# A linear-attention kernel with its layers: an empty GpSimd instruction in the drain's place, and the state's update in another visit

## The chip, the cores and the metric

One core of a Trainium2 chip. The metric is device time in microseconds (us) for one call; lower is better. The kernel before took 424.89 us (median of three runs, 424.53 to 431.61).

## The reference, cut to what matters

Inputs are float32 and already drawn: four batches, eight heads, 768 tokens, 48 features per head. First comes a recurrent attention with a decaying state, then three layers whose maximum is taken, then an output layer.

```
for t in range(S):
    cur = einsum('bhd,bhe->bhde', u[None] * kt, vt)
    y[:, :, t] = einsum('bhd,bhde->bhe', rt, state + cur)
    state = wt[:, :, :, None] * state + einsum('bhd,bhe->bhde', kt, vt)
...
h = max(max(x @ w1, x @ w2), x @ w3)      # 3072 x 384 by 384 x 768
return h @ w_out                          # 768 x 384
```

## The kernel before, in words

**Two streams of work share TensorE.** The attention runs over 24 chunks of 128 tokens (six chunks per batch). The layers run over six halves of 512 tokens. Four chunks make the input of one half, so the attention of half h+1 runs while the layers of half h do.

**The layers** (`moe_groups`) come in groups of nine matmuls, 26 groups to a half: 18 of L147 (six feature blocks by w1, w2, w3; each feeds one PSUM bank, tile `psm`) and 8 of L167 (the output layer). `take_up` frees a bank: for w1 ScalarE copies it (L126), for w2 and w3 VectorE takes the maximum (L129). It is written one group late: the take-up of a group stands in its engine's queue behind what was written while that group and the gap after it were emitted. The pool `ps_m` has three banks, and a new tile gets the bank that was freed longest ago, in the order of the program.

**The attention** is a list of lettered steps, one chunk at a time; the string `ORD` (L71) orders them for chunks 4 to 23. A digit after a letter is how many chunks ahead the step works, `|` ends a unit, and one unit is emitted after nearly every layer group. The letters that matter here:

- R (`from_state`, L450): state times r, into the tile y. V (`values`, L489): half of the values, added into y. Z (`values2`, L489 again): the other half, which adds into the same banks from the other half of the array's rows; a TensorE drain (L482) stands before it. E (`result`, L503): ScalarE copies y into x.
- X (`scores`, L417): the next chunk's products into the tiles `gram`. M: VectorE takes them into `a`.
- T (`transposes`, L437): four transposes of the next chunk's keys into the one bank of the pool `ps_tu`, and a ScalarE copy of it to `kn` (L439), of which there is one.
- U (`to_state`, L460): keys times values into the same bank of `ps_tu`, read from `kn`. S (`state`, L473 and L475): VectorE forms the next state from it. Every sixth chunk (5, 11, 17, 23) ends a batch and has no U and no S, and the chunk after it starts from no state.
- b, f, r, c: the decays and what they scale, two chunks ahead (VectorE L335, L345, L356, L357; c is a ScalarE Square in place over what r reads, L362). d, e: the diagonal, two chunks ahead (GpSimd L373, L374, then VectorE L387 and GpSimd L393). n: a load.

So before the change a chunk has one long visit to TensorE (R, X, V, U, drain, Z), one short one four groups later (T), and VectorE's S, r and ScalarE's c between them. All engines run their own instructions in the order written (`manual_schedule`). From half 1 on the layers split their input into two fp32r parts on ScalarE and VectorE (`x_parts`, L106 and L107), emitted near the end of the half before; in half 1 the weights are split as well (`fix`); from half 2 on every second group carries a check of one weight block (L307 on VectorE, L309 on ScalarE).

Of the kernel before, what the change touches and what calls it, by code (L numbers as in the profile page):

```python
# [29 lines left out]
F32 = mybir.dt.float32  # L30
# [10 lines left out]
B, H, S, D = 4, 8, 768, 48  # L41
DM, FF = 384, 768
NP = 4
C = 128
# [6 lines left out]
HT = 512  # L51
HC = C // 2
CPH = HT // C
# [14 lines left out]
FRONT = "n2 w U0 b1 | d1 f1 r1 | w e1 c1 S0 W4 X1 T1 | R0 M0 | V0 Z0 E0 |"  # L68
LAST = "R0 M0 | V0 Z0 E0 n2 w U0 W9 n3 | b1 d1 | f1 r1 w | e1 c1 S0 X1 T1 R1 |"
TURN = "b1 d1 w | f1 w | r1 c1 | e1 M0 w | "  # L70
ORD = "w R0 X1 V0 U0 Z0 E0 b2 d2 | f2 n3 w | S0 r2 c2 | e2 M1 w | T1 w | |"  # L71


START = ("aaaaaaaaaaaacaaacaccaxmcacmcamcamcamcamcamcamcamcaamca"
# [10 lines left out]
def lines(n):  # L85

    return -(-n // LINE) * LINE
# [3 lines left out]
def kernel(ctx: ExitStack, tc, tin, nat, u_flat, u_pair, v_t, w_all, out, ytr):  # L91
    nc = tc.nc
# [83 lines left out]
    with ExitStack() as fast:  # L176
# [15 lines left out]
        ps_tu = pool("ps_tu", 1, space=PSUM)  # L192
        ps_m = pool("ps_m", 3, space=PSUM)
# [4 lines left out]
        natt = {}  # L198
# [230 lines left out]
        def goes_on(k):  # L429
            return k % NCH < NCH - 1  # L430

        def transposes(k):
            if goes_on(k):
                p = prep[k]
                pt = ps_tu.tile([128, 512], F32, name="tu")
                for pr in range(NP):
                    nc.tensor.transpose(pt[:, pr * 112:pr * 112 + 112], p["kp"][0:112, pr, :], ident[0:112, 0:112])  # L437
                p["kn"] = kn = kn_p.tile([128, lines(NP * 112)], F32, name="kn")[:, 0:NP * 112].rearrange("p (a b) -> p a b", a=NP)
                nc.scalar.copy(out=kn[:, :, :].rearrange("p a b -> p (a b)"), in_=pt[:, 0:NP * 112])  # L439
# [27 lines left out]
        def state(k):  # L467

            if goes_on(k):
                new = prep[k]["pu"][0:112, 0:NP * D].rearrange("p (a b) -> p a b", a=NP)  # L470
                if k % NCH > 0 and k >= CPH:
# [3 lines left out]
                nc.vector.tensor_tensor(out=sstar[(k + 1) % 2][0:112, :, 0:D], in0=new,  # L475
                                        in1=dec[(k + 1) % 2][0:112, :].unsqueeze(2).broadcast_to([112, NP, D]), op=ALU.mult)

        def values(k, second=False):
            p = prep[k]
            fresh = k % NCH == 0 and not second  # L480
            if second:
                nc.tensor.drain()  # L482
            for late in range(2):
                for row in range(2):
                    for half, m in ((0, 64), (1, 48)):
                        hh, j = row ^ second, (1 - row) ^ late
                        h, lo = 4 * half + 2 * j + hh, 64 * row
                        a = p["a"][lo:lo + HC, 2 * hh + half]
                        nc.tensor.matmul(p["y"][64 * half:64 * half + m, hh, j, HC * late:C],  # L489
                                         lhsT=natt[k][0][lo:lo + HC, h * D:h * D + m],  # L490
                                         rhs=a[:, j, :] if late else a[:, j::2 - j, :],
                                         start=fresh and not late, stop=True, skip_group_check=True)

        def values2(k):
            values(k, True)

        def result(k):
# [7 lines left out]
            for lo in (0, 64) if slot == CPH - 1 else ():  # L505
                for j in range(KT):
                    eng = nc.scalar if lo and half < PLAIN else nc.sync
                    eng.dma_start(out=x[lo + 48:lo + 64, j, :], in_=x[lo + 16 * j:lo + 16 * j + 16, KT, :])

        steps = dict(X=scores, M=take, T=transposes, R=from_state, U=to_state, S=state, V=values, Z=values2, E=result, n=load,  # L510
                     b=prep_scan_b, f=prep_scan_f, r=prep_rk, c=prep_check, d=prep_diag1, e=prep_diag2)
        ready = {("n", k) for k in range(3)}
# [16 lines left out]
        def attn():  # L529
            for step in "bdfeWrXTcW":  # L530
                ahead(step, 0) if step != "W" else warmer(2 if ("X", 0) in ready else 8)
            for k in range(NK):
                if k == CPH:
                    nc.scalar.dma_start(out=u_bc[:, :], in_=u_flat.partition_broadcast(128))
                for step in (FRONT if k < CPH - 1 else LAST if k < CPH else TURN + ORD if k == CPH else ORD).split():
                    if step == "|":
# [134 lines left out]
    with tc.If(verdict[0] != 0, label="general"), ExitStack() as slow:  # L671
# [9 lines left out]
        with tc.For_i(0, B) as b:  # L681
            for pr in range(NP):
# [18 lines left out]
                for j in range(KT):  # L701
                    with tc.For_i(0, 16) as i:
# [16 lines left out]
                        for q in range(2):  # L719
                            z = ps_z.tile([2, S // 2], F32, name="z")  # L720
                            nc.tensor.matmul(z[:, :], lhsT=sel[0:112, :], rhs=kv[0:112, q * (S // 2):(q + 1) * (S // 2)],
                                             start=True, stop=True)
                            nc.vector.tensor_copy(out=yo[:, q * (S // 2):(q + 1) * (S // 2)], in_=z[:, :])
                        for hh in range(2):
                            place, lo = 2 * hh + pr % 2, 64 * (pr // 2)
# [8 lines left out]
        for i in range(NW if w_all.dtype != F32 else 0):  # L734
# [3 lines left out]
            lo, hi = words[:, :, 0], words[:, :, 1]  # L738
# [93 lines left out]
```

## Time and profile before

| | |
|---|---|
| median of three runs | 424.89 us |
| the profiled execution, its own time | 423.95 us |
| its span, first to last instruction | 422.2 us |
| mean granted TensorE clock in it | 0.995 |
| TensorE busy, weight loads busy | 408.9 us (97%), 320.9 us (76%) |
| VectorE, ScalarE, GpSimd busy | 272.0, 151.9, 74.3 us |
| matmuls of the layers L147 and L167, share of the chain that ended last | 55% and 17% |

The busy share of TensorE counts matmuls whose ends are modelled, so the distance from one start to the next says more than a duration. An fp32 matmul shows as two rows. "issue" as a releaser means that an engine waited for nothing that the profile shows. PE is TensorE's matmuls, PEld its weight loads, DVE VectorE, ACT ScalarE, POOL GpSimd.

### The profile page before, as it was taken

What the parts mean: (1) busy time and instruction counts of PE and PEld (TensorE: products, weight loads), DVE (VectorE), ACT (ScalarE), POOL (GpSimd) and SP (SyncE); (2) the same over time, 40 slices, a digit from 0 to 9 for tenths busy, and PEclk for the clock granted to TensorE, in tenths of its full rate; (3) what the DMA queues carried; (4) which work ended last, traced back from release to release, by engine and by line L of the source; (5) the groups of instructions that cost most, each with busy time, mean ns of one, the idle gap of its engine ahead of it and who ended that gap; (6) DMA issues with size and microseconds to landing.
All of it is one profiled execution on the core that took longest, in us unless ns stands there. A gap on an engine that the chain in (4) does not pass through costs nothing.

```text
span 422.2 us, 9012 instructions
## 1 busy us (share of the span) xinstructions
PE 408.9 (97%) x3695; PEld 320.9 (76%) x3695; DVE 272.0 (64%) x515; ACT 151.9 (36%) x318; POOL 74.3 (18%) x92
## 2 busy tenths in 40 slices
PE   6989999999999999999999999999999999999995
PEld 3665545556678888987888988888988888988895
DVE  5988789877769977835867658658547624223320
ACT  1334344232554443424425455334523221312111
POOL 3120111030443140313023113113113100000000
PEclk9989999999999999999999999999999999999999
DMA  8835975244172403295735496653280000200002
GB/s 224 258 100 151 351 250 168 68 168 124 44 231 67 123 7 118 48 283 173 219 92 182 114 279 209 198 180 94 52 265 23 2 2 0 79 18 0 1 2 78
DMA packets 20702, 53.27 MB, mean 126 GB/s; under 512 B 2816, under 2 KB 9088, under 8 KB 20656
## 3 DMA queue, kind: packets, MB, share of 16 engines
q1 hardware_dynamic: 16832, 42.61, 33.3%
q10 hardware_dynamic: 3824, 10.03, 7.6%
q8 instruction: 30, 0.49, 0.5%
q14 instruction: 16, 0.13, 0.1%
HBM read 46.74 MB, written 4.72 MB: 122 GB/s over the span
## 4 chain that ended last, share of the span: by engine, by line
PE 92%; DVE 4%; issue 1%; DMA 1%; ACT 1%; POOL 0%; POOLq 0%; DVEq 0%; ACTq 0%
PE psm L147 55%; PE psm L167 17%; PE y L489 5%; PE gram L417 4%; PE y L450 3%; PE tu L460 3%; PE psm L526 2%; PE tu L437 2%; PE psm L383 1%; DMA out_dram<-m 1%; DVE tin L356 1%; DVE tin L357 1%; DVE gf L345 1%; DVE gf L335 1%; DVE x_lo L107 0%
## 5 line engine op out<-in xcount | busy, mean ns | idle before, releaser
L147 PE MATMUL psm<-x_hi,w 128*128 128x512 f32 x540 | 172.9, 394 | 0.6 <-ACT m L126 0.6
L147 PEld LDWEIGHTS psm<-x_hi,w 128*128 128x128 f32 x540 | 101.4, 188 | 22.5 <-ACT m L126 0.8
L147 PE MATMUL psm<-x_lo,w 128*128 128x512 f32 x270 | 105.3, 390 | 0.0
L129 DVE TENSOR_TENSOR m<-psm,m 128x512 f32<-128x512 f32 x60 | 41.2, 687 | 58.6 <-PE psm L147 52.6
L167 PE MATMUL psm<-w,h_hi 128*128 128x384 f32 x288 | 78.0, 364 | 0.0
L393 POOL TENSOR_SCALAR_AFFINE_SELECT a<-cs 64x512 f32<-64x512 f32 x48 | 35.5, 739 | 233.7 <-DVE cs L387 117.2
L147 PEld LDWEIGHTS psm<-x_lo,w 128*128 128x128 f32 x270 | 50.7, 188 | 9.9
L167 PEld LDWEIGHTS psm<-w,h_hi 128*128 128x128 f32 x288 | 51.8, 188 | 6.4
L147 PE MATMUL psm<-x,w 128*128 128x512 f32 x108 | 48.3, 598 | 0.0
L503 ACT COPY x<-y 112x512 f32<-112x512 f32 x24 | 14.1, 587 | 74.4 <-PE y L489 74.0
L167 PE MATMUL psm<-w,h_lo 128*128 128x384 f32 x120 | 40.2, 335 | 0.0
L362 ACT ACTIVATE gf<-gf 112x1034 f32<-112x1034 f32 x24 | 25.7, 1070 | 36.3 <-DVE tin L357 33.0
L106 ACT CAST h_hi<-m 128x512 fp32r<-128x512 f32 x30 | 18.7, 622 | 54.6 <-DVE m L129 54.6
L335 DVE TENSOR_TENSOR_SCAN gf<-tin,d_bwd 112x517 f32<-112x517 f32 x24 | 31.1, 1296 | 10.0 <-DMA tin<-in_tin_dram 10.0
L147 PEld LDWEIGHTS psm<-x,w 128*128 128x128 f32 x108 | 19.9, 190 | 22.8 <-issue 22.1
L107 DVE TENSOR_TENSOR h_lo<-m,h_hi 128x512 fp32r<-128x512 f32 x30 | 22.2, 740 | 19.0 <-ACT h_hi L106 19.0
L345 DVE TENSOR_TENSOR_SCAN gf<-tin,d_fwd 112x517 f32<-112x517 f32 x24 | 29.6, 1235 | 0.8
L489 PE MATMUL y<-a,v 64*64 64x128 f32 (+3 forms) x768 | 25.5, 248 | 2.9
L489 PEld LDWEIGHTS y<-a,v 64*64 64x64 f32 (+1 forms) x768 | 20.5, 126 | 6.0 <-issue 5.9
L373 POOL TENSOR_TENSOR kr<-kr 128x384 f32<-128x384 f32 x16 | 18.7, 1170 | 26.8 <-DMA kr<-in_nat_dram 25.8
L426 DVE COPY_PREDICATED a<-mask,gram 128x384 f32<-128x384 int32 x44 | 23.2, 582 | 0.0
L126 ACT COPY m<-psm 128x512 f32<-128x512 f32 x30 | 17.5, 582 | 15.9 <-PE psm L147 13.6
(71 smaller groups left out, 427.9 us busy)
## 6 DMA issues: line engine op xcount, KB each, us to landing
tin<-in_tin_dram SPq DMA_DIRECT2D x23, 677.7 KB, 5.5
w<-in_w_all_dram SPq DMA_DIRECT2D x24, 384.0 KB, 6.6
cv<-in_w_all_dram ACTq DMA_DIRECT2D x24, 384.0 KB, 3.3
kr<-in_nat_dram SPq DMA_DIRECT2D x16, 384.0 KB, 5.9
v<-in_nat_dram SPq DMA_DIRECT2D x24, 192.0 KB, 5.5
out_dram<-m SPq DMA_DIRECT2D x24, 192.0 KB, 2.3
x<-x SPq DMA_DIRECT2D x33, 32.0 KB, 2.0
tin<-in_tin_dram SPq DMA_DIRECT2D x1, 258.0 KB, 4.8
```

The lines of the kernel that those rows point to most:

```text
L106: nc.scalar.copy(out=hi, in_=src)
L107: rest = lambda: nc.vector.tensor_tensor(out=lo, in0=src, in1=hi.bitcast(F32), op=ALU.subtract)
L129: nc.vector.tensor_tensor(out=m[:, :], in0=ps[:, :], in1=m[:, :], op=ALU.max)
L147: nc.tensor.matmul(ps[:, :], lhsT=wt[f * 3 + wi][:, ct * 128:(ct + 1) * 128], rhs=xt[:, ct, :], start=(n == 0), stop=(n == KT * len(terms) ...
L167: nc.tensor.matmul(pss[tt][:, 0:DM], lhsT=ht[f][:, tok], rhs=wt[FT * 3 + f][:, :], start=(f == 0 and i == 0), stop=(f == FT - 1 and i == l ...
L335: nc.vector.tensor_tensor_scan(out=gf[0:112, 0, ::-1], data0=t[0:112, 0:WC][:, ::-1], data1=d_bwd[0:112, ::-1], initial=0.0, op0=ALU.mult, ...
L345: nc.vector.tensor_tensor_scan(out=gf[0:112, 1, :], data0=tbuf[k % NB][0:112, 0:WC], data1=d_fwd[0:112, :], initial=0.0, op0=ALU.mult, op1 ...
L362: nc.scalar.activation(out=flat, in_=flat, func=AF.Square, accum_out=acc[0:112, k:k + 1])
L373: nc.gpsimd.tensor_tensor(out=n[:, 0, :], in0=n[:, 0, :], in1=n[:, 1, :], op=ALU.mult)
L393: nc.gpsimd.affine_select(out=a[rows, :, 0:2, :], pattern=[[0, 4], [0, 2], [1, HC]], in_=cs[rows, :].rearrange("p (a b) -> p a b", b=2).un ...
L426: nc.vector.copy_predicated(out=p["a"][:, 2 * hh:2 * hh + 2, :, :].rearrange("p a b c -> p a (b c)"), mask=mask_b(2), data=p["gs"][hh].rea ...
L489: nc.tensor.matmul(p["y"][64 * half:64 * half + m, hh, j, HC * late:C], lhsT=natt[k][0][lo:lo + HC, h * D:h * D + m], rhs=a[:, j, :] if la ...
```

## The change

For chunks 4 to 23 the drain is left out. Instead GpSimd gets an empty instruction that waits for the last matmul of V, and the first matmul of Z waits for it. X moves between V and Z. U moves from the long visit to the unit that holds S, r and c, and T moves there too, two units earlier than it was. From chunk 5 on T takes a bank of the layers' pool, so that U and T need not share one.

```
-ORD = "w R0 X1 V0 U0 Z0 E0 b2 d2 | f2 n3 w | S0 r2 c2 | e2 M1 w | T1 w | |"
+ORD = "w R0 V0 X1 Z0 E0 b2 d2 | f2 n3 w | U0 T1 S0 r2 c2 | e2 M1 w | w | |"
...
         def transposes(k):
...
-                pt = ps_tu.tile([128, 512], F32, name="tu")
+                pt = ps_m.tile([128, HT], F32, name="psm") if k > CPH else ps_tu.tile([128, 512], F32, name="tu")
...
+        def after(later, sooner):
+            how = mybir.DependencyInfo(mybir.DependencyClass.Sync, mybir.DependencyReason.DATA)
+            tc.add_manual_dep(later.ins, sooner.ins.name, how, reason="the second values use the first's banks")
+            return later
...
         def values(k, second=False):
...
-            if second:
+            if second and k < CPH:
                 nc.tensor.drain()
...
-                        nc.tensor.matmul(p["y"][64 * half:64 * half + m, hh, j, HC * late:C],
+                        mm = nc.tensor.matmul(p["y"][64 * half:64 * half + m, hh, j, HC * late:C],
...
+                        if "first" in p:
+                            after(mm, p.pop("first"))
+            if not second and k >= CPH:
+                p["first"] = after(nc.gpsimd.nop(nofuse=True), mm)
```

## Rows read from the trace of the kernel before

**Rows 1.** The page, busy time: us (share of the span) xinstructions of each engine.
```profile
PE 408.9 (97%) x3695; PEld 320.9 (76%) x3695; DVE 272.0 (64%) x515; ACT 151.9 (36%) x318; POOL 74.3 (18%) x92
```
**Rows 2.** Waits of the whole span: us in total, times, longest.
```profile
PEld y L489 <- issue: 5.9, 24, 0.3
```
**Rows 3.** Timeline of TensorE, chunk 9's long visit: start, duration, work.
```profile
138.20 0.39 PE L147 MATMUL psm<-x_hi,w 128*128 128x512 f32 x1
138.52 0.66 PE L450 MATMUL y<-tin,sstar 48*64 48x128 f32 x16
139.02 0.84 PE L417 MATMUL gram<-tin 48*64 48x128 f32 x32
139.68 0.50 PE L489 MATMUL y<-a,v 64*48 64x128 f32 x16
140.12 0.67 PE L460 MATMUL tu<-v,kn 128*64 128x48 f32 x16
140.90 0.56 PE L489 MATMUL y<-a,v 64*64 64x128 f32 x16
141.39 0.50 PE L147 MATMUL psm<-x_hi,w 128*128 128x512 f32 x1
```
**Rows 4.** Timeline of the weight loads in the same visit, around the drain.
```profile
140.11 0.54 PEld L460 LDWEIGHTS tu<-v,kn 128*64 128x64 f32 x16
140.90 0.42 PEld L489 LDWEIGHTS y<-a,v 64*64 64x64 f32 x16 [0.24 <-issue]
```
**Rows 5.** Timeline of TensorE, chunk 11's visit, which has no U.
```profile
171.43 1.18 PE L489 MATMUL y<-a,v 64*48 64x128 f32 x32
172.54 0.62 PE L167 MATMUL psm<-w,h_hi 128*128 128x384 f32 x2
```
**Rows 6.** The chain that ended last, around chunk 13's T: start, us, line.
```profile
204.23 8.39 PE psm L147 x36
212.62 0.39 PE tu L437 x4
213.00 6.14 PE psm L147 x27
```
**Rows 7.** Timelines of VectorE and ScalarE, chunk 13: S, the Square, the take-up.
```profile
207.40 0.35 DVE L473 TENSOR_TENSOR scur<-tu,sstar 112x192 f32<-112x192 f32 x1
...
209.46 1.07 ACT L362 ACTIVATE gf<-gf 112x1034 f32<-112x1034 f32 x1 [0.95 <-DVE tin L357]
...
210.52 0.57 ACT L126 COPY m<-psm 128x512 f32<-128x512 f32 x1
```
**Rows 8.** Timelines of ScalarE and TensorE, chunk 12: a group that waited for its bank.
```profile
196.36 0.57 ACT L126 COPY m<-psm 128x512 f32<-128x512 f32 x1
...
196.98 0.50 PE L147 MATMUL psm<-x_hi,w 128*128 128x512 f32 x1 [0.62 <-ACT m L126]
```
**Rows 9.** Timelines of three engines, chunk 15 to the start of half 3.
```profile
235.76 0.36 DVE L473 TENSOR_TENSOR scur<-tu,sstar 112x192 f32<-112x192 f32 x1 [0.66 <-PE tu L460]
...
240.78 0.48 ACT L171 COPY m<-psm 128x384 f32<-128x384 f32 x1 [0.43 <-PE psm L167]
241.16 0.65 ACT L309 ACTIVATE cv<-cv,mid_top 128x384 f32<-128x384 uint32 x1
...
242.92 1.67 ACT L106 CAST x_hi<-x 128x512 fp32r<-128x512 f32 x3 [1.03 <-DMA x<-x]
...
244.64 0.39 PE L147 MATMUL psm<-x_hi,w 128*128 128x512 f32 x1
```
**Rows 10.** Timelines: GpSimd to TensorE, TensorE to ScalarE, and GpSimd's diagonal for chunk 16.
```profile
2.92 0.20 POOL L521 MEMSET warm<- 128x128 bf16 x1
3.17 0.13 PEld L526 LDWEIGHTS <-warm 128*128 128x128 bf16 x2 [3.17 <-POOL warm L521]
...
141.53 0.59 ACT L503 COPY x<-y 112x512 f32<-112x512 f32 x1 [3.15 <-PE y L489]
...
212.10 1.08 POOL L373 TENSOR_TENSOR kr<-kr 128x384 f32<-128x384 f32 x1
```

More of the change, by code (lines that the diff above doesn't have):

```diff
@@ L488, in values @@
                         a = p["a"][lo:lo + HC, 2 * hh + half]
-                        nc.tensor.matmul(p["y"][64 * half:64 * half + m, hh, j, HC * late:C],
-                                         lhsT=natt[k][0][lo:lo + HC, h * D:h * D + m],
-                                         rhs=a[:, j, :] if late else a[:, j::2 - j, :],
-                                         start=fresh and not late, stop=True, skip_group_check=True)
+                        mm = nc.tensor.matmul(p["y"][64 * half:64 * half + m, hh, j, HC * late:C],
+                                              lhsT=natt[k][0][lo:lo + HC, h * D:h * D + m],
+                                              rhs=a[:, j, :] if late else a[:, j::2 - j, :],
+                                              start=fresh and not late, stop=True, skip_group_check=True)
+                        if "first" in p:
+                            after(mm, p.pop("first"))
+            if not second and k >= CPH:
+                p["first"] = after(nc.gpsimd.nop(nofuse=True), mm)
         def values2(k):
```

## The prediction

> **What bounds the kernel now.** I read the page's busy times first: TensorE is busy for 97% of the span, with VectorE at 64% and GpSimd at 18% [rows 1], and the chain that ended last runs through TensorE's own instructions nearly everywhere. So a microsecond of TensorE's issue time is a microsecond of the kernel, and anything on another engine counts only where it makes TensorE wait. Next the waits: in front of the values' matmuls the weight loads stood still 24 times, 5.9 us together, with nothing else to blame [rows 2]. There are 24 chunks and one drain in each, so a drain costs 5.9 / 24 = 0.25 us of weight loading. Then the timeline of one visit, where starts are to be compared with starts: R to X 0.50, X to V 0.66, V to U 0.44, U to Z 0.78, Z to the layers 0.49 [rows 3]. U's own loads began at 140.11 and Z's at 140.90, with 0.24 of standstill before the latter [rows 4], so U issues for 0.54 and the rest is the drain. A layer matmul takes 6.14 / 27 = 0.227 us, and T costs 0.39 between two groups [rows 6].
>
> **The drain out.** Chunk 11 has V, drain and Z with nothing between: 172.54 - 171.43 = 1.11 from V to the layers [rows 5]. Without a drain V and Z would take 0.44 + 0.49 [rows 3], so the drain costs 0.18 of issue there; by its standstill it is 0.25 [rows 2]. I take 0.22. Chunks 4 to 22 lose it: 19 x 0.22 = 4.2 us, with ends 3.4 and 4.8.
>
> **The empty instruction in.** No row shows such an instruction on GpSimd. Its loop is: V's last matmul ends (by the model 0.50 after V's start [rows 3]); a waiting engine starts 0.07 later (Z ends at 140.90 + 0.56 = 141.46, ScalarE starts at 141.53 [rows 3, 10]); the instruction itself takes between nothing and the 0.20 of a real memset; TensorE starts 0.05 after GpSimd (3.12 to 3.17) [rows 10]. That is 0.62 to 0.82 after V's start. X now stands in that place and keeps TensorE issuing until 0.44 + 0.66 = 1.10 [rows 3]. So the wait costs nothing, with X as its cover and 0.28 us or more to spare. Chunk 23 has no X: its Z waits 0.18 to 0.38 beyond V's 0.44, where the drain cost 0.18 to 0.25. That is a loss of 0.1, between a gain of 0.1 and a loss of 0.2.
>
> On GpSimd's queue the diagonals (L373, L374) now stand behind the empty instruction. They ran far ahead of their visit: the one written in chunk 14's visit started at 212.10, some 7 us before it [rows 10]. Now they start with V and take some 2.3 us, and their reader on VectorE is written three layer groups later, 3 x 2.05 = 6.1 us. Nothing is lost. Ahead of the empty instruction stands only the select of the unit before last, long done. U and T issue no DMA, so no step passes a transfer on SP. But the load of v three chunks on reuses the v that U reads, and it is written one unit after U's new place: SP's queue may stand at it until U instead of Z, some 4 us longer, and behind it wait the next chunk's loads and the layers' stores, none of which is due before the next visit. I cost that at nothing. The units' letters w only load weights that have all been asked for by then.
>
> **U and T moved.** Their issue time stays: U 0.54, T 0.39. What changes is seams. Gone are T's entry from a layer group (nothing to be seen: it costs 0.39 in all [rows 6]) and V to U (0.44, shorter than Z's 0.49 [rows 3], so nothing either). New are layer to U and U to T. Nearest is layer to R: 138.52 - 138.20 = 0.32 where the next layer matmul would have come after 0.227, so 0.09 [rows 3]. For the two seams together I take 0.05, between T's nothing and R's 0.09 at each (0 to 0.19), on 15 chunks: 0.75 us, from 0 to 2.9.
>
> **VectorE held up.** This is the price I trust least. S waits for U on VectorE's queue, and r, the diagonal's sum, M and the layers' take-ups queue behind it; c and take-ups queue behind r on ScalarE. Take chunk 13. Before, S ran at 207.40, while TensorE was still in the group before this unit, since U was long done; c began at 209.46 and the take-up of that group at 210.52, ending at 211.09 [rows 7]. That group began 2.05 us after the visit's first, so it ended at 204.23 + 0.11 + 4.1 = 208.44 [rows 6]. After the change all of TensorE comes 0.78 us earlier there (U's 0.54 and the drain), so it ends at 207.66, U's result is there at about 208.5, and S starts 1.1 later than before; the take-up ends at 212.2. Who needs the bank? The pool gives the bank freed longest ago, and T's own bank comes back with its quick copy, so the order of waiting is: the next group takes the bank of the group two before the unit (free since about 206.4), the second group T's bank, the third this one. U and T end at 208.6, so the third group starts at 208.6 + 4.1 = 212.7. It is covered by 0.5 us. Before, a group that had no such cover shows the mechanism: in chunk 12 the take-up ran at 196.36 and the group three later stood for 0.62 us [rows 8].
>
> Where the cover is thinner I count a loss: chunk 12, whose stall ends at a fixed moment, so that its own gain of 0.2 is lost; chunks 8 and 9, where the weights' splits stand in the same queues, 0.1 each; and the starts of halves 3 and 4. At chunk 15 S began at 235.76 and x_hi at 242.92, and the new half at 244.64 [rows 9]. Now U follows the fifth output group, S starts at about 239.5, c (2.06 behind S by [rows 7]) at 241.6, and after c's 1.07 come a copy of 0.48 and a check of 0.65 and more [rows 9]. So x_hi starts at 244.0, its first third is split at about 245.2, where the half would want it at 244.6: 0.6 us, for chunks 15 and 19. In all 0.2 + 0.2 + 1.2 = 1.6 us, from 0 to 5 (0.5 at each of the seven chunks like 13, and the 1.6).
>
> **The sum.** -4.2 + 0.1 + 0.75 + 1.6 = -1.75 us, so 423.95 becomes 422.2 for an execution like the profiled one; the median of the runs lies 0.94 above that execution, so I forecast 423.1 us.
>
> **A rule weighed against the trace.** At chunk 9 the switch from V's 64-row tiles to U's 128-row tiles shows no gap, while U to Z, a switch and a drain, shows 0.24 [rows 3, 4]; chunk 11, a drain alone, costs 0.18 [rows 5]. So the drain owns the gap. The Trainium skill (TensorEngine Tiling (Array Packing), Key Properties) says that a change of tiling mode itself drains TensorE. By that rule U to Z would have stood still without any drain, and only chunks 5, 11 and 17, which have no U, gain. The trace bears this out badly at V to U, but it shows no U to Z without a drain.
>
> **The rivals.**
>
> - *The switch was the cost.* Only the three chunks without U gain: -0.6 + 0.1 + 0.75 + 1.6 = +1.85, so 426.7; with the late work at nothing 425.1. For it: U to Z has both causes at once. Against it: the 0.18 at chunk 11 and the free switch from V to U. Chance 0.12.
> - *Covered altogether.* ScalarE and VectorE catch up and the seams are free: -4.2 to -4.8, so 420.1 to 420.7. For it: VectorE idles for a third of the span [rows 1]. Chance 0.22.
> - *Slower: the late S starves the layers of banks.* The place is the second layer group after the unit. If it got this group's bank and not T's, it would start at 208.6 + 2.05 = 210.65 and wait until 212.2, 1.6 us, at chunks 8, 9, 12, 13, 16, 20 and 21, and some 0.4 at three others: 12.4 - 4.2 + 0.85 = +9, so 434. If the order holds but S's delay is a microsecond longer than I count, the third group waits 0.5 at each and the halves' starts more: 427 to 430. It decides where the delay of 1.1 exceeds 1.6 us. Against it: the pool's order, and 0.5 us of cover. Chance 0.11 (0.07 for over 2%).
> - *The change doesn't do what it says:* the wait for GpSimd takes the drain's place, if the loop takes 0.5 us more than I make it. Then Z stands as long as before: +0 to +2, 425 to 427. Chance 0.07.
>
> **How the numbers follow.** The forecast, 421 to 424.8, has the remaining 0.48. From 420 to 427 lie the forecast, the first two rivals but for an edge, and the fourth: 0.85 less the runs' own scatter, so I give 420.0 to 427.0. A change of 2% (8.5 us) is about what a measurement of this kernel tells from none. Faster by that needs twice the whole drain: 0.02. Slower by that needs the third rival's wrong bank or a loop through GpSimd of a microsecond: 0.08. Within: 0.90.
>
> **What would show it.** The standstill before L489 falls from 5.9 us over 24 to about 1 over 4, and X to Z shows no wait for GpSimd. From V to the layers there is 0.44 + 0.66 + 0.49. VectorE's S shows a wait for U in nearly every chunk, and TensorE's waits for take-ups and for x_hi grow from 0.6 to about 2 us. I am wrong if Z waits for GpSimd after X, if the seam around U exceeds 0.2, or if the second layer group after T waits for a take-up.

## The result and the profile after

The changed kernel took 425.02 us (median of four runs, 418.71 to 431.43), the kernel before 428.06 us beside it. The ratio is 0.9868, 95% interval 0.9823 to 0.9913: the same by a bound of 2%, and a little faster. A second comparison, of 13 runs, gave 0.9925 (0.9903 to 0.9947), about 3 us. Two of the four runs of either kernel were disturbed (430.53 and 431.43 us for the changed one, 431.61 and 431.23 for the other), and the comparisons leave such runs out, so the medians say less than the ratios do.

The profiled execution took 419.51 us with a span of 417.7, 4.5 us less than before's. Not all of that is the change's. The first layer matmul, ahead of which only the opening and four chunks that the change leaves alone are run, starts at another time. Timelines of TensorE, the kernel before and then the changed one:

```profile
39.06 1.96 PE L147 MATMUL psm<-x,w 128*128 128x512 f32 x4
```

```profile
37.22 3.67 PE L147 MATMUL psm<-x,w 128*128 128x512 f32 x8
```

That is 1.84 of the 4.5 us. (The stretch behind the last layer matmul took back 0.4 us: 4.50 before, 4.90 after, and between 4.4 and 5.3 over the kernels below.) The windows (stretch, length, TensorE's busy time, granted clock as a share of 2.4 GHz, DMA share, GB/s) show a clock that differed, first before and then after:

```profile
10.00:25.00 15.00, 13.66 (x190) 0.91 0.63 196
```

```profile
10.00:25.00 15.00, 11.77 (x225) 1.00 0.68 206
```

The granted clock of this stretch was 0.91 in one execution and 1.00 in the other. Over the profiles of this case the first layer matmul comes between 37.1 and 48.4 us. In the four late ones (after_again, nop_only, t_back and bare_loop below, 45.1 us and more) the clock from 25 to 37 us was 0.50, the lower of its two levels (1.2 GHz), where it was 0.96 to 1.00 in the others. Here is after_again's:

```profile
25.00:37.00 12.00, 11.79 (x146) 0.50 0.46 142
```

From 50 to 400 us it was 1.00 in every profile. I therefore measure from the start of the first layer matmul to the end of the last: **378.66 us before, 375.59 and 375.43 after** in two executions, though the second had its first layer matmul at 47.01. The change is worth **3.1 to 3.2 us**.

The page after, busy times, against [rows 1]:

```profile
PE 404.1 (97%) x3695; PEld 315.7 (76%) x3695; DVE 274.2 (66%) x515; ACT 151.8 (36%) x318; POOL 78.5 (19%) x92
```

The waits after (engine, tile, line, releaser: us in total, times, longest), against [rows 2]; V and Z now stand on L495, the empty instruction on L502:

```profile
POOL kr L373 <- PE y L495: 81.9, 16, 8.6
...
DVE scur L473 <- PE tu L460: 21.2, 10, 4.0
...
PEld y L495 <- issue: 1.7, 6, 0.4
...
PEld y L495 <- POOLq L502: 0.3, 1, 0.3
...
PE psm L147 <- DVE x_lo L107: 0.4, 2, 0.2
...
PE psm L147 <- ACT x_hi L106: 0.2, 1, 0.2
...
PE psm L147 <- ACT kn L439: 0.2, 1, 0.2
```

The standstill in front of V and Z fell from 5.9 us to 1.7; four of its six are those of chunks 0 to 3, which keep the drain. GpSimd's diagonals and VectorE's S now wait for TensorE at length, as forecast. Of that, what reaches TensorE are the waits for x_lo and x_hi at the starts of halves 3 and 4 (below). For the empty instruction only one load stood still, 0.3 us, at chunk 23.

Chunk 9 after, TensorE, the visit and then the unit with U and T, against [rows 3]:

```profile
135.13 0.39 PE L147 MATMUL psm<-x_hi,w 128*128 128x512 f32 x1
135.45 0.66 PE L450 MATMUL y<-tin,sstar 48*64 48x128 f32 x16
135.94 0.50 PE L495 MATMUL y<-a,v 64*48 64x128 f32 x16
136.27 0.84 PE L417 MATMUL gram<-tin 48*64 48x128 f32 x32
136.94 0.51 PE L495 MATMUL y<-a,v 64*48 64x128 f32 x16
137.38 0.50 PE L147 MATMUL psm<-x_hi,w 128*128 128x512 f32 x1
...
141.36 0.39 PE L147 MATMUL psm<-x_hi,w 128*128 128x512 f32 x1
141.68 0.67 PE L460 MATMUL tu<-v,kn 128*64 128x48 f32 x16
142.28 0.60 PE L437 MATMUL psm<-ident,tin 112*128 112x112 f32 x4
142.65 0.48 PE L147 MATMUL psm<-x_hi,w 128*128 128x512 f32 x1
142.97 0.40 PE L147 MATMUL psm<-x_lo,w 128*128 128x512 f32 x1
```

Starts against starts, to the next step's start: R 0.49, V 0.33, X 0.67, Z 0.44. The visit is 1.93 us, where it was 2.87 [rows 3]; U adds 0.60 in its own place. In chunk 11, which has no U, the changed visit is again 1.93 (R at 166.84 below, layers at 168.77), before some 2.3: X now fills what was a drain between V and Z [rows 5].

```profile
166.84 0.66 PE L450 MATMUL y<-tin,sstar 48*64 48x128 f32 x16
...
168.34 0.50 PE L495 MATMUL y<-a,v 64*64 64x128 f32 x16
168.77 0.61 PE L167 MATMUL psm<-w,h_hi 128*128 128x384 f32 x2
```

The start of half 3 after, all engines, against [rows 9]. S waits 3.63 us for U, c ends late, and x_hi and x_lo are not there when TensorE comes:

```profile
234.71 0.36 DVE L473 TENSOR_TENSOR scur<-tu,sstar 112x192 f32<-112x192 f32 x1 [3.63 <-PE tu L460]
...
236.77 1.07 ACT L362 ACTIVATE gf<-gf 112x1034 f32<-112x1034 f32 x1 [1.01 <-DVE tin L357]
...
239.40 1.66 ACT L106 CAST x_hi<-x 128x512 fp32r<-128x512 f32 x3 [0.46 <-ACT cv L309]
239.56 0.34 PE L167 MATMUL psm<-w,h_lo 128*128 128x384 f32 x1
...
240.07 0.50 PE L147 MATMUL psm<-x_hi,w 128*128 128x512 f32 x1 [0.17 <-ACT x_hi L106]
...
240.80 0.50 PE L147 MATMUL psm<-x_lo,w 128*128 128x512 f32 x1 [0.22 <-DVE x_lo L107]
...
241.13 0.62 PE L147 MATMUL psm<-x_hi,w 128*128 128x512 f32 x2
```

By starts it costs more than the 0.17 and 0.22 that are called waits. An output matmul is followed 0.17 later and a layer matmul 0.23 later where nothing holds them up; here the three steps from 239.56 on take 0.51, 0.73 and 0.33, together 0.94 too much.

### The profile page after: what moved, and what is told of

The parts are those of the page before. It is cut to its first block, busy times and chain, and to the rows that moved or that the text cites. A ratio compares the mean times of both kernels' runs of the same rounds, so it can differ in the third digit from the quotient of the medians.

```text
span 417.7 us, 9006 instructions
## 1 busy us (share of the span) xinstructions
PE 404.1 (97%) x3695; PEld 315.7 (76%) x3695; DVE 274.2 (66%) x515; ACT 151.8 (36%) x318; POOL 78.5 (19%) x92
## 4 chain that ended last, share of the span: by engine, by line
PE 87%; DVE 5%; DMA 4%; ACT 2%; issue 1%; ACTq 0%; SPq 0%; DVEq 0%; POOLq 0%
PE psm L147 55%; PE psm L167 16%; PE y L495 4%; PE gram L417 3%; PE y L450 3%; PE tu L460 2%; DMA cv<-in_w_all_dram 2%; PE psm L437 2%; DMA tin<-in_tin_dram 1%; PE psm L383 1%; DMA out_dram<-m 1%; PE psm L536 1%; DVE gf L345 1%; DVE tin L356 1%; DVE tin L357 1%
## 5 line engine op out<-in xcount | busy, mean ns | idle before, releaser
L373 POOL TENSOR_TENSOR kr<-kr 128x384 f32<-128x384 f32 x16 | 22.5, 1404 | 81.9 <-PE y L495 81.9
L345 DVE TENSOR_TENSOR_SCAN gf<-tin,d_fwd 112x517 f32<-112x517 f32 x24 | 33.0, 1377 | 0.8
L335 DVE TENSOR_TENSOR_SCAN gf<-tin,d_bwd 112x517 f32<-112x517 f32 x24 | 30.0, 1248 | 4.1 <-DMA tin<-in_tin_dram 4.1
L495 PE MATMUL y<-a,v 64*48 64x64 f32 (+3 forms) x768 | 24.7, 245 | 0.6
L495 PEld LDWEIGHTS y<-a,v 64*48 64x48 f32 (+1 forms) x768 | 21.2, 126 | 3.7 <-issue 1.7
```

Source lines behind the costliest of these rows:

```text
L335: nc.vector.tensor_tensor_scan(out=gf[0:112, 0, ::-1], data0=t[0:112, 0:WC][:, ::-1], data1=d_bwd[0:112, ::-1], initial=0.0, op0=ALU.mult, ...
L345: nc.vector.tensor_tensor_scan(out=gf[0:112, 1, :], data0=tbuf[k % NB][0:112, 0:WC], data1=d_fwd[0:112, :], initial=0.0, op0=ALU.mult, op1 ...
L373: nc.gpsimd.tensor_tensor(out=n[:, 0, :], in0=n[:, 0, :], in1=n[:, 1, :], op=ALU.mult)
L495: mm = nc.tensor.matmul(p["y"][64 * half:64 * half + m, hh, j, HC * late:C], lhsT=natt[k][0][lo:lo + HC, h * D:h * D + m], rhs=a[:, j, :] ...
```

## The experiments

Each edit is given against the changed kernel. "Layers" is the distance from first to last layer matmul; ratios are to the kernel before. The distance leaves the openings out; the ratios hold them.

| kernel | layers, us | against before's 378.66 | ratio, 95% interval |
|---|---|---|---|
| changed, run again | 375.43 | -3.2 | 0.9925 (0.9903 to 0.9947) |
| nop_only | 375.25 | -3.4 | 0.9932 (0.9903 to 0.9961) |
| drain_kept | 381.62 | +3.0 | 1.0061 (1.0036 to 1.0086) |
| u_earlier | 375.29 | -3.4 | 0.9871 (0.9806 to 0.9936) |
| mixed | 373.69 | -5.0 | 0.9901 (0.9870 to 0.9933) |
| u_in_visit | 372.94 | -5.7 | 0.9858 (0.9842 to 0.9874) |
| t_back | 375.53 | -3.1 | one run only |
| bare_loop | 382.43 | +3.8 | one run only |
| memset_512 | 381.70 | +3.0 | one run only |
| u_in_visit_fetch | 371.42 | -7.2 | 0.9853 (0.9810 to 0.9895) |

**after_again**, the changed kernel once more, without an edit.

> The changed kernel, unaltered, against the kernel before on one chip. The two profiles differ by 4.5 us, but 1.84 us of that stand ahead of the first layer matmul (39.06 against 37.22 us), where the program is the same. Theory A (the change is worth about 3 us, the rest was chance in the start): 2.5 to 4 us below before in the timed runs (0.6% to 1%), and the first layer matmul starts anywhere between 37 and 39.5 us. Rival B (the start is quicker because of the change): the first layer matmul again near 37.2 us, and 4.5 to 5.5 us (1.1% to 1.3%) below before.

It gave the second ratio, inside theory A's 0.6% to 1%, and showed that the layers' distance repeats to 0.16 us. The opening does not: the first layer matmul, at 47.01, came far later than either theory had it.

**nop_only**: the order and the banks of before, and only the drain replaced.

```diff
-ORD = "w R0 V0 X1 Z0 E0 b2 d2 | f2 n3 w | U0 T1 S0 r2 c2 | e2 M1 w | w | |"
+ORD = "w R0 X1 V0 U0 Z0 E0 b2 d2 | f2 n3 w | S0 r2 c2 | e2 M1 w | T1 w | |"
...
-                pt = ps_m.tile(...) if k > CPH else ps_tu.tile(...)
+                pt = ps_tu.tile([128, 512], F32, name="tu")
```

> The order of before, T in its old bank, and only the drain replaced by the empty GpSimd instruction. Theory A (the drain owned the standstill): U to Z falls from 0.78 to 0.54 us at the 16 chunks that have U; at chunks 5, 11, 17 and 23 Z waits for the instruction with nothing in between and gains little. In all 16 x 0.24 = 3.8 us below before. Rival (the switch from U's 128-row tiles to Z's 64-row tiles was the cost): U to Z stays at 0.75 us or more, and the time is that of before within 0.5 us.

All that the whole change gives is here, 375.25. TensorE in chunk 9:

```profile
145.37 0.67 PE L460 MATMUL tu<-v,kn 128*64 128x48 f32 x16
145.97 0.56 PE L495 MATMUL y<-a,v 64*64 64x128 f32 x16
146.46 0.50 PE L147 MATMUL psm<-x_hi,w 128*128 128x512 f32 x1
```

U to Z is 0.60, where it was 0.78 [rows 3]: the drain owned 0.18 there, and not the 0.24 that the theory had.

The 0.60 holds a second cost. A row's tile, such as 128*64, is the part of the array that a matmul uses, rows by columns. R, V, X and Z stay within 64*64, U takes 128*64, T and the layers take (nearly) 128*128. Compare where the next group starts with the modelled end of the group ahead, its start plus its duration. Between groups of one kind of tile it starts 0.17 us before that end (V to X and X to Z, chunk 9 after). Where the kind changes, it starts only 0.06 to 0.07 before (V to U in [rows 3], U to T and Z to the layers after, U to Z here). Behind a drain it starts 0.11 to 0.13 after that end, whether the kind changes (U to Z in [rows 3]) or not (X to Z in drain_kept, below). So a change of tile costs some 0.10 us and a drain some 0.30, and a drain that stands at a change costs only the 0.18 that the change has not cost already.

The rule that the prediction weighed (the Trainium skill, TensorEngine Tiling (Array Packing), Key Properties) is that a change of tiling mode drains TensorE. These rows agree that such a change costs time, about a third of what the explicit drain costs; whether the array empties at it, no run here shows.

**drain_kept**: the order and the banks of after, with the drain for every chunk and no empty instruction.

```diff
-            if second and k < CPH:
+            if second:
...
-            if not second and k >= CPH:
-                p["first"] = after(nc.gpsimd.nop(nofuse=True), mm)
```

> The order and banks of the changed kernel, but the drain still in front of Z, and no GpSimd instruction. Theory A (the drain is where the gain came from, the move costs): X to Z rises from 0.67 to about 0.95 us at 20 chunks, so 5 to 7 us above the changed kernel and 1 to 3 us above before. Rival (the new order is what gained): within 1 us of the changed kernel.

The drain kept, the new order makes the kernel 3.0 us slower than before. TensorE in chunk 9, with the drain between X and Z:

```profile
139.74 0.84 PE L417 MATMUL gram<-tin 48*64 48x128 f32 x32
140.71 0.56 PE L495 MATMUL y<-a,v 64*64 64x128 f32 x16
```

X to Z is 0.97 and not 0.67. Behind X, where the tiles don't change, a drain costs 0.30; behind U, where they do, it cost 0.18.

**bare_loop**: X stands ahead of V again, and nothing between V and Z.

```diff
-ORD = "w R0 V0 X1 Z0 E0 ...
+ORD = "w R0 X1 V0 Z0 E0 ...
```

> The changed kernel with X ahead of V again, so that nothing covers the way from V over GpSimd to Z (U and T stay moved). Theory A (at chunk 23, where nothing covers it, V to Z took 0.70 us instead of V's own 0.33): V to Z 0.70 us at every chunk, 0.37 us x 19 = 7 us above the changed kernel, 382 to 383 us from the first layer matmul to the last, above before. Rival (GpSimd's answer is quick enough to hide behind V's own tail): within 2 us of the changed kernel.

TensorE in chunk 9:

```profile
147.40 0.50 PE L495 MATMUL y<-a,v 64*48 64x128 f32 x16
148.06 0.56 PE L495 MATMUL y<-a,v 64*64 64x128 f32 x16 [0.15 <-POOLq L502]
```

V to Z takes 0.66: the loop through GpSimd, by itself (0.65 at chunk 23 of the changed kernel, which the expectation had at 0.70). It lies inside the 0.62 to 0.82 that the prediction put together from hops. The kernel loses 6.8 us against the changed one, as expected, and stands 0.8 us above drain_kept. So the uncovered loop is no cheaper than a drain; it is a wait that another step can cover.

**memset_512**: a real GpSimd instruction in the empty one's place.

```diff
...
-                p["first"] = after(nc.gpsimd.nop(nofuse=True), mm)
+                p["first"] = after(nc.gpsimd.memset(pad[:, :], 0.0), mm)
```

> The changed kernel, but in place of the empty GpSimd instruction stands a real one, a memset of 128x512 fp32 that nothing reads; the order of TensorE's work is untouched. It tests the cover: the theory is that the loop TensorE, GpSimd, TensorE costs nothing only because X's matmuls stand beside it. In chunk 9 of the changed kernel V starts 0.33 before X and X lasts 0.67, so Z is due 1.00 us after V's start; the loop with the empty instruction takes 0.66 (V to Z in the kernel with the loop uncovered), and a memset of this size some 0.5 us more (an estimate), 1.1 to 1.2. Theory: Z comes 0.1 to 0.2 us late in each of 19 chunks, 2 to 4 us in all, from first to last layer matmul 377.5 to 379.5 against 375.5 of the changed kernel, with TensorE's waits now showing GpSimd. Rival (the loop was never close to deciding, the cover has room to spare): 375.5 as in the changed kernel and no wait of TensorE for GpSimd.

381.70 lies 2.2 us above the theory's range: slower than it said, but its way. TensorE and GpSimd in chunk 9, where L503 is the memset:

```profile
139.45 0.50 PE L496 MATMUL y<-a,v 64*48 64x128 f32 x16
...
139.78 0.84 PE L418 MATMUL gram<-tin 48*64 48x128 f32 x32
140.12 0.52 POOL L503 MEMSET pad<- 128x512 f32 x1 [4.29 <-PE y L496]
...
140.70 0.56 PE L496 MATMUL y<-a,v 64*64 64x128 f32 x16
```

V to Z is now 1.25: 0.67 until the memset starts, 0.52 of it and 0.06 until Z, against the 1.00 at which Z was due. The loop decides as soon as it is longer than V and X; the rival (room to spare) falls. The room was 1.00 - 0.66 = 0.34 us.

**u_earlier** and **mixed**: U and T one unit earlier, in all chunks and from chunk 12 on.

```diff
-... | f2 n3 w | U0 T1 S0 r2 c2 | e2 M1 w | w | |
+... | f2 n3 w U0 T1 | S0 r2 c2 | e2 M1 w | w | |
```

> The changed kernel with U and T one unit earlier (after f, n instead of ahead of S), so that S no longer waits for U on VectorE. Theory A (S held up by U starves the starts of halves 3 and 4 and chunk 12's bank): the waits of TensorE for x_lo and for copies ahead of L147 vanish, VectorE's 21 us of waiting for U go below 3, and the kernel is 0.8 to 1.5 us below the changed one. Rival (those stalls come from elsewhere): the same time as the changed kernel within 0.5 us.

> The changed kernel's order for chunks 4 to 11, and from chunk 12 on U and T one unit earlier. Counted from the first layer matmul to the last (before 378.7 us, changed 375.6 and 375.4, U and T earlier throughout 375.3). Theory A (the earlier place loses 0.4 us at each of the chunks 8 and 9, where the weights' splits stand in the queues, and wins 0.9 and 0.4 us at the starts of halves 3 and 4): 374.4 to 374.7 us, 1% below before in the timed runs. Rival (those losses and gains are not tied to the chunks): 375.2 us or more.

At u_earlier the stretches of chunks 15 and 19 lost their excess: -0.18 us against before in each, where the changed kernel has +0.74 and +0.26. So U's late result does cause what the halves' starts lose. But chunks 8 to 10 came out 0.33 above before, not 0.50 below (a layer matmul waits 0.15 for ScalarE's copy at chunk 8 and again at 9), and the sum stayed: the 0.8 to 1.5 us that the theory promised did not come. With the changed order up to chunk 11 and the earlier one behind it, mixed has both gains, and at chunks 11 and 12, where no layer matmul waits any longer, 0.5 us more than the profiled changed kernel: 373.69, below the expected 374.4 to 374.7.

**t_back**: T back in its old unit and bank, U left in the new one.

```diff
-... | U0 T1 S0 r2 c2 | e2 M1 w | w | |
+... | U0 S0 r2 c2 | e2 M1 w | T1 w | |
...
```

> The changed kernel with only T put back to its own unit and to the state's bank; U stays ahead of S. Theory A (T's seams are small, S still waits for U): the stalls at the starts of halves 3 and 4 stay, and U and T apart cost 0 to 0.15 us a chunk more, 375.5 to 378 us from the first layer matmul to the last. Rival (T's place in the layers' banks is what starves them): the stalls go, below 374.7 us.

375.53, the changed kernel's time. T's move and the layers' bank for it are worth nothing either way.

**u_in_visit**: U back in the visit, behind Z; T as in t_back.

```diff
-ORD = "w R0 V0 X1 Z0 E0 b2 d2 | f2 n3 w | U0 T1 S0 r2 c2 | e2 M1 w | w | |"
+ORD = "w R0 V0 X1 Z0 U0 E0 b2 d2 | f2 n3 w | S0 r2 c2 | e2 M1 w | T1 w | |"
...
```

> The drain replaced and X between V and Z as in the changed kernel, but U stays in the long visit, behind Z, and T stays alone in its old place and bank. Theory A (U costs some 0.75 us of TensorE wherever it stands, since its 128-row tiles differ from its neighbours'; what the move brings is only that S has to wait): 374.3 to 375 us from the first layer matmul to the last, no waits for x_lo, and S never waits for U. Rival (merging U with T saves a seam): 0.2 us more at each of 15 chunks, 377 us or more with the stalls taken off.

It beats both kernels, and by 1.4 us the theory's range, so U does not cost 0.75 us wherever it stands. TensorE, chunk 9, and then chunk 12 where it stops:

```profile
137.28 0.50 PE L495 MATMUL y<-a,v 64*48 64x128 f32 x16
...
138.28 0.50 PE L495 MATMUL y<-a,v 64*48 64x128 f32 x16
138.72 0.67 PE L460 MATMUL tu<-v,kn 128*64 128x48 f32 x16
139.31 0.50 PE L147 MATMUL psm<-x_hi,w 128*128 128x512 f32 x1
...
194.58 0.50 PE L147 MATMUL psm<-x_hi,w 128*128 128x512 f32 x1 [1.35 <-ACT m L126]
```

The visit with U is 2.52 us (R at 136.79), 0.35 less than before. U behind Z costs 0.59, one change of tile included: a chunk now has three such changes (layer to R, Z to U, U to layer), where before, nop_only, t_back and the changed kernel each have four. The stop of 1.35 is a transfer's, as VectorE's queue shows in the same chunk:

```profile
190.96 0.36 DVE L307 TENSOR_SCALAR cv<-cv 128x384 uint32<-128x384 uint32 x1 [3.51 <-DMA cv<-in_w_all_dram]
```

The check of a weight block waits for its load; S, r, c and the take-up stand behind it.

**u_in_visit_fetch**: u_in_visit, and those loads asked for earlier.

```diff
+            if half == CHECK - 1 and g == GPH - 2 and w_all.dtype != F32:
+                while len(checks) < 3:
+                    fetch_w()
```

> The kernel with the update back in the values' visit and the empty instruction kept (u_in_visit, 372.9 us from first to last layer matmul), with one edit: the weight checks that chunk 12 needs first have their DMAs issued at the end of half 1 and not on the spot. In u_in_visit chunk 12 stops once for 1.35 us behind ScalarE's m product, whose own operand came late by DMA. Theory (that stall is a late transfer and not part of the order): it vanishes and nothing takes its place, 371.5 to 372 from first to last layer matmul, a ratio of about 0.984 to the kernel before. Rival (the stall only moves, to a bank or to the next transfer on the same queue): 372.9 as before, ratio 0.986, with another wait of 1 us or more in chunks 11 to 13.

371.42, 0.1 below the theory's range; the stop is gone and no other came. The ratio, 0.9853, cannot tell this from u_in_visit's 0.9858 (its interval is 0.9810 to 0.9895). It is the best of the kernels run: 7.2 us below before between the first layer matmul and the last.

## Why the prediction was right, and which terms were off

The time between two visits (R to R), predicted by the terms of the sum and measured, after less before, in us:

| chunks | predicted | measured |
|---|---|---|
| 4 to 7 | -0.73 | -1.09 |
| 8 to 10 | -0.31 | -0.50 |
| 11, 12 | -0.19 | -0.89 |
| 13, 14 | -0.34 | -0.41 |
| 15, start of half 3 | +0.43 | +0.74 |
| 16 to 18 | -0.56 | -0.71 |
| 19, start of half 4 | +0.43 | +0.26 |
| 20 to 22 | -0.51 | -0.63 |
| 23 to the end | +0.10 | +0.15 |
| sum | -1.7 | -3.1 |

The median, 425.02, lies inside the range of 420.0 to 427.0 and in "within 2%", but that it does is in part luck: the profiled execution, 419.51, lies below the range, its opening 1.84 us shorter than before's. What the change itself is worth puts the profiled execution between the forecast and *Covered altogether*: 423.95 - 3.07 = 420.9, a tenth below the forecast's own 421 to 424.8.

**The drain out: right, and mis-sized.** The term of 0.22 came from V at 0.44 and Z at 0.49. Both were taken beside U: V's 0.44 holds the change to U's tile, which the prediction read as free (V starts X after 0.33), and Z behind X takes 0.44. So chunk 11's drain cost 1.11 - 0.33 - 0.44 = 0.34 (with 0.05 by which Z takes longer behind it) and not 0.18, and the visit got shorter by 0.94 us and not by 0.76 (U's 0.54 and 0.22), and by some 0.35 where there is no U.

**The empty instruction in: right.** X covers it, chunk 23 pays about what the drain cost (V to the layers 1.14 after, 1.11 before), and GpSimd's later diagonals delay nobody. The rival *The change doesn't do what it says* is a matter of cover: in bare_loop and in memset_512 it came true.

**U and T moved: mis-sized.** I took 0.05 for the seams, the time that a move between two groups costs beyond their own issue. T alone, in u_in_visit_fetch (chunk 12, TensorE):

```profile
192.49 0.39 PE L147 MATMUL psm<-x_hi,w 128*128 128x512 f32 x1
192.72 0.55 PE L437 MATMUL tu<-ident,tin 112*128 112x112 f32 x4
193.04 0.47 PE L147 MATMUL psm<-x_hi,w 128*128 128x512 f32 x1
193.35 0.39 PE L147 MATMUL psm<-x_lo,w 128*128 128x512 f32 x1
```

From the last layer matmul ahead to the second behind is 0.86 us here and 1.61 with U in chunk 9 above. U in the new unit therefore costs 0.75, where it cost 0.59 behind Z in u_in_visit: 0.16 more, at the upper end of 0 to 0.19. Most of it is one more change of tile, some 0.10: in the new unit the tile changes into U and again into T, while U behind Z adds one change only. With the drain's term this gives 0.94 - 0.75 = 0.19 gained by a chunk with nothing else in it, where the prediction had 0.17. That they agree is luck: two errors of about 0.17 cancel. The first was not confined to chunks with U, which is why 5, 11 and 17 gained more than forecast.

**VectorE held up: right at the halves' starts, wrong at chunk 12, nothing at 8 and 9.** The starts were put at 0.6 each. Against an ordinary chunk's -0.19 they measure 0.93 and 0.45, 1.4 in all for the 1.2. Chunk 12 is the failed step. "Its own gain is lost" took the stall [rows 8] for a bank late by the order of take-ups. It began with a DMA. ScalarE's request for the first weight blocks and VectorE's check in chunk 12, before and then after:

```profile
185.24 1.58 ACTq L299 DMA_DIRECT2D cv<-in_w_all_dram  x3
...
193.36 0.36 DVE L307 TENSOR_SCALAR cv<-cv 128x384 uint32<-128x384 uint32 x1 [2.78 <-DMA cv<-in_w_all_dram]
```

```profile
181.45 1.32 ACTq L299 DMA_DIRECT2D cv<-in_w_all_dram  x3
...
188.49 0.36 DVE L307 TENSOR_SCALAR cv<-cv 128x384 uint32<-128x384 uint32 x1 [2.54 <-DMA cv<-in_w_all_dram]
```

Before, S, r, c (from 195.29) and the copy of [rows 8] stand in the queues behind this check. After the change the check runs 4.87 us earlier, and chunk 11's R only 3.42 (170.26 and 166.84), so the check gained 1.45 on TensorE. The stall did not end at a fixed moment: a layer matmul's wait of 0.22 was left of the 0.62 in the profiled execution, and none in after_again. What was left stands behind the same load, for ScalarE's copy of T comes behind the check (TensorE, chunk 12 after):

```profile
190.62 0.50 PE L147 MATMUL psm<-x_hi,w 128*128 128x512 f32 x1 [0.22 <-ACT kn L439]
```

So chunks 11 and 12 gained 0.89 us in one execution and 1.06 in the other. That the load's date decides is shown by u_in_visit_fetch, for u_in_visit's stop. Of the 1.45, 0.37 is the load's place: it was asked for 14.98 us behind chunk 11's R before and 14.61 after. The other 1.08 is the transfer: from the request to the check 8.12 and 7.04. Why that was shorter stays open; over the runs it took 5.6 to 8.4.

**The rivals.** *The switch was the cost* falls as it was put: in nop_only 0.18 of the 0.28 behind U went with the drain. But a change of tile does cost some 0.10, and the prediction had it at nothing. *Covered altogether* was half right: covered, but for the halves' starts and with seams. *Late S starves the layers of banks*: S does wait, and no layer matmul waited for a layer's take-up; the order of banks held. The one that waited for a bank, at chunk 12, is the second group after T, which the prediction named as a sign of being wrong; it got T's bank, as the prediction's order says, and T's copy was late by the load.

**By its parts**: the drain's place under X with U kept in the visit gives -5.7 us, U's own place takes back 2.6 (u_in_visit against t_back), T's place and bank nothing that shows in the sum. The 2.6 is net of u_in_visit's stop, which t_back does not have; against u_in_visit_fetch it is 4.1.

## What to carry to other kernels

A drain taken out for a wait on another engine gains only what work stands beside that wait; count the loop (0.66 us here) and the cover (1.00) from the first step's start. Keep small steps in one visit, ordered by the part of the array that they use: a step of 0.59 us moved out of its visit paid 0.16 more each time, most of it for one more change of tile, and what reads it came late at the starts of two halves. Price a seam from a pair without a change: V's 0.44, taken as V's own, hid 0.11. And when a stall names an engine, follow that engine's queue back until something names a DMA.

## What was not expected of the hardware

The opening varies more than the change is worth: with the same work, the first layer matmul started between 37.07 and 48.43 us, with a granted clock of 0.50 from 25 to 37 us in the late ones. From there on the layers' distance repeated to 0.2 us. A change of tile between small groups of matmuls costs some 0.10 us here, at every kind of change that the rows show. A drain had no single price: 0.18 behind U, where the tile changes anyway, 0.30 behind X.
